# Pooled attention with a gated MLP: a bank read ahead of two sums in the last two tiles, and a sum and a load put behind the rows of x in the second tile

## Chip, core and metric

The kernel runs on one core of a Trainium2 chip. The time is the device time in microseconds (us) of one launch. Before the change nine runs had a median of 287.71 us (287.24 to 288.73).

## What is computed

The reference takes q, k and v of 8 batches, 8 heads, 576 positions and 64 channels. Keys and values are averaged over groups of 8 positions, so each head has 72 pooled keys. The result x of the attention has 4608 rows (batch by position) and 512 columns (head by channel), and goes through a gated two-layer MLP:

```
k_p = k.reshape(B, H, Sp, 8, D).mean(axis=3);  v_p likewise
attn = softmax(q @ k_p^T / sqrt(D))
x = (attn @ v_p), as 4608 rows x 512
h = x @ w_in            # 512 -> 2048
g = h * cos(h)
out = g @ w_out         # 2048 -> 512
```

## The kernel before

**Tiles.** The MLP runs over nine tiles of 512 rows, t = 0 to 8. While tile t is in the MLP, TensorE also does the attention of batch b = t + 1, whose result tile t + 1 reads. So tiles 1 to 6 are "steady" (`steady` is b < 8), tile 7 has only the last 64 rows of batch 7 left to do (`rest`), and tile 8 has none. The schedule is manual: each engine runs its instructions in the order in which the program issues them.

**Up part of a tile.** Eight groups of eight matmuls (L353) multiply the columns of `xT` (x transposed) with `w_in` into PSUM banks. For each group ScalarE takes the cosine (L363) and VectorE multiplies it with h (L367) into `g_sb`. The groups go through the banks in the order 0, 2, 1, the two output banks, 0, 2, 1, 0.

**Down part.** From tile 1 on, the product with `w_out` is made by seven half-size products instead of eight (a Strassen-like scheme), `product(0)` to `product(6)`, 16 matmuls each (L431). They need four sums of quarters of g, `put_g(1..4, i)` (L397), each in two halves i, made by VectorE: `g1` and `g3` from `g_sb`, `g2` from `g1`, `g4` from `g2`. Every product accumulates in one of two banks, A (`obanks[1]`) or Bb (`obanks[0]`; in the last tile each of them is a pair of banks, so that the two halves of the rows can be read one by one). Products alternate between the two: 0, 2, 4, 6 in A, and 1, 3, 5 in Bb. After each product `reads[i]` empties its bank, `reads[0]` by a copy to `p_sb` (L445; VectorE, in tiles 7 and 8 ScalarE), the others by an addition on VectorE (L447). Products 2 and 3 begin a new sum in their bank, so product 2 waits for `reads[0]` (and for g2), and product 3 for `reads[1]` (and for g1). Product 4 needs g3, product 5 needs g4. In tile 8 each read issues its two output DMAs for each half of the rows; in the other tiles the output DMAs come in the next tile.

**Attention in a steady tile.** The batch's first 384 rows go in three chunks u0, u1, u2. `values_rows` multiplies the exponentials with the pooled values (L295), takes reciprocals (L298) and makes the rows of x (`x_rows`, L300) on VectorE, and SyncE issues a DMA that transposes them into `xT` (L304). The next tile's first matmul waits for all three. The chunk u3 and the last 64 rows (`values`, L268 to L279) follow later in the tile.

**GpSimd.** At the end of tile t it pools the keys and then the values of batch b + 1 with `pool_first` (four additions, L156) and `pool_rest` (two additions, L162, and the writes to `ring`, L165, or to `vz`, L168). The second half for the values, `pool_rest(b, "v")`, stands in the next tile's up part. It also issues the loads: the keys of batch b + 2 by `load_kv` (L115) between the two halves of the pooling of the keys, and the q and v of the batch after next in the up part (L96, L115), behind a one-element copy `gate` (L589) that waits for the transposed keys `kk`. A second `gate` (L712), which waits for `put_g(4, 1)`, stands ahead of the pooling. SyncE issues the transposes of q (L206) and of the pooled keys (L192) in the up part too.

The order in the down part, which the change edits, is that of L664 to L681:

```
product(1, 2)
if t == 1:
    put_g(2, 0)
put_gs((1, 1), (2, 1))
reads[0]()
put_gs((3, 1), (4, 1))
reads[1]()
if t == 1:
    put_g(4, 0)
if steady:
    values_rows(*u0)
product(2)
reads[2]()
```

Of the kernel before, what the change touches and what calls it, by code (L numbers as in the profile page):

```python
# [20 lines left out]
def kernel(  # L21
# [10 lines left out]
    B, H, S, D = q.shape  # L32
# [119 lines left out]
    def pool_first(b, which):  # L152

        x, s = staged.pop((which, b)), half_sums
        for h in range(0, H, 2):
            nc.gpsimd.tensor_tensor(out=s[:, h:h + 2], in0=x[:, h:h + 2, 0:4, :], in1=x[:, h:h + 2, 4:8, :], op=ADD)  # L156
# [60 lines left out]
    def ex_col(u, i):  # L217

        (c0, n), (h0, nh) = u
        return (i // 2 % 2 * (nh // 2) + i // 4 * 2 + i % 2) * n  # L220
# [66 lines left out]
    def values_rows(b, u, pair):  # L287

        (c0, n), (h0, nh) = u
        ex = att.pop(("ex", b, u))  # L290
        ps = pair.rearrange("p b n -> p (b n)").rearrange("p (j w) -> p j w", w=2 * 128)
        for i in range(nh):
            pj, hp = divmod(i, 2)
            v_and_sum = vz[b % 2].rearrange("p j a d -> p j (a d)")[:, pj, hp * (3 * D - 1):hp * (3 * D - 1) + D + 1]
            nc.tensor.matmul(ps[0:n, pj, hp * (D + 1):(hp + 1) * (D + 1)], lhsT=ex[:, ex_col(u, i):ex_col(u, i) + n],  # L295
                             rhs=v_and_sum)
        inv = asb.tile([128, KCH, 2], FP32, name="inv_rows", tag="inv_rows", bufs=2)
        nc.vector.reciprocal(out=inv[0:n], in_=ps[0:n, :, D:D + 2])  # L298
        x = asb.tile([128, d_model], BF16, name="x_rows", tag="x_rows", bufs=4)
        nc.vector.tensor_tensor(  # L300
            out=x[0:n].rearrange("p (j a d) -> p j a d", j=KCH, a=2),
            in0=ps[0:n, :, 0:2 * (D + 2)].rearrange("p j (a w) -> p j a w", a=2)[:, :, :, 0:D],
            in1=inv[0:n].unsqueeze(3).to_broadcast([n, KCH, 2, D]), op=mybir.AluOpType.mult)
        nc.sync.dma_start_transpose(out=xT[:, :, b * S + c0:b * S + c0 + n], in_=x[0:n])  # L304
# [94 lines left out]
    def put_gs(*kis):  # L399
        for k, i in kis:  # L400
            put_g(k, i)
# [159 lines left out]
    for t in range(NT):  # L561
        b = t + 1
        if t > 0:

            for fp in up_order(t)[0:2]:
                up_mm(t, fp, 0, 2)
        for n, fp in enumerate(up_order(t)):
            up_mm(t, fp, 2 if n < 2 else 0)
            between = ()
            if t == 0:  # L570
                if fp == 4:
                    puts = pool_k_mm(1, obanks[0], 0, 2), pool_k_mm(1, obanks[1], 2, 4)
                elif fp in (5, 6):
                    g0 = 9 * (fp - 5)
                    puts = q_transpose_mm(1, obanks[0], g0, g0 + 5), q_transpose_mm(1, obanks[1], g0 + 5, g0 + 9)
                if fp in (4, 5, 6):
                    puts[0](vec)
                    between = ((puts[1], act),)
            up_g(t, fp, between)
            if 0 < t and 3 <= n < 6:  # L580
                put_gs(*[(k, 0) for k in (((3,), (1,), ()) if t == 1 else ((1, 2), (3,), (4,)))[n - 3]])
            if 0 < t and b < B:
                if n == 0:
                    q_transpose(b)
                    k_transpose(b)
                elif n == 2:
                    pool_rest(b, "v")
                    if b + 1 < B:
                        nc.gpsimd.tensor_copy(out=gate, in_=kk[b % 2][0:1, H - 1, 0:1])  # L589
                        load_q(b + 1)  # L590
                        load_kv(b + 1, "v", v)
            if n == 2:
                while stores:
                    stores.pop(0)()
        mms = [(ms, fc) for ms in range(4) for fc in range(FFCH)]
        if t == 0:
            mms = [(ms, fc) for hm in range(2) for cg in (0, 2, 1, 3) for ms in range(2 * hm, 2 * hm + 2)
                   for fc in range(4 * cg, 4 * cg + 4)]


        def S_(n, bank):
            return lambda: scores(b, us[n], banks[bank])

        later = []

        def V_(n, bank, wait=None):
            return lambda: values(b, us[n], banks[bank], wait)

        fill = []
        if t < B:  # L610
            exp_tables()
            fill = [(1, lambda: scores(t, REST, banks[2])), (16, lambda: values(t, REST, banks[1]))]
        if t == 0:
            fill = [(2, fill[0][1]), (2, S_(0, 0)), (8, lambda: pool_v_mm(1, banks[1])),
                    (8, lambda: values(t, REST, banks[2])), (8, S_(1, 0)), (8, V_(0, 1)),
                    (18, S_(2, 2)), (21, V_(1, 0, later)), (26, S_(3, 1)), (32, lambda: later.pop()()),
                    (32, V_(2, 2)), (40, V_(3, 0))]
        if t == FIRST:
            early_inverses.clear()
        if t < FIRST:  # L620
            fi = 0
            for n, (ms, fc) in enumerate(mms):
                while fi < len(fill) and fill[fi][0] <= n:
                    fill[fi][1]()
                    fi += 1
                down_mm(obanks[ms % 2], ms, fc)
                if fc == FFCH - 1:
                    down_out(t, ms, obanks[ms % 2])
                if n == 4:
                    put_weights(0, nc.vector, (1,))  # L630
                elif n == 36:
                    put_weights(1, nc.vector, (3,))
            put_weights(1, nc.vector, (2, 4))
        else:
            products, reads = down_products(t)

            def product(i, j=0, k=2 * HF):
                for mm in products[i][j:k]:
                    mm()

            later = []

            u0, u1, u2, u3 = [(b, CHUNKS[i], banks[j]) for i, j in enumerate((2, 1, 0, 1))]
            ur = (t, REST, banks[2])

            def scores_of(*parts):
                for part in parts:
                    scores_mm(*part)
                for part in parts:
                    scores_exp(*part)  # L650

            def muls():
                while later:
                    later.pop(0)()

            steady, rest = b < B, t < B
            if rest:
                exp_tables()
            product(0)
            product(1, 0, 2)  # L660
            if steady:
                scores_of(u0, u1, u2)
            elif rest:
                scores_of(ur)  # L664
            product(1, 2)
            if t == 1:
                put_g(2, 0)
            put_gs((1, 1), (2, 1))
            reads[0]()
            put_gs((3, 1), (4, 1))  # L670
            reads[1]()
            if t == 1:
                put_g(4, 0)
            if steady:
                values_rows(*u0)
            product(2)
            reads[2]()
            if steady:
                values_rows(*u1)
                values_rows(*u2)  # L680
            product(3)  # L681
            reads[3]()
            muls()
            product(4)
            reads[4]()
            muls()
            if steady:
                scores_of(ur, u3)
            product(5, 0, 4)
            if rest:  # L690
                values(*ur, later)
            product(5, 4, 12)
            muls()
            if steady:
                values_rows(*u3)
            product(5, 12)
            reads[5]()
            muls()
            product(6)
            reads[6]()  # L700
        if t < B:
            sin_tables()
        if b + 1 < B:
            if t == 0:
                load_kv(b + 1, "k", k)
                load_q(b + 1)
                load_kv(b + 1, "v", v)
                put_weights(0, nc.gpsimd, (3, 2, 4))
                put_weights(1, nc.gpsimd, (1,))
            else:  # L710

                nc.gpsimd.tensor_copy(out=gate, in_=g4[0:1, HF - 1, 0:1])  # L712
            pool_first(b + 1, "k")
            if b + 2 < B:
                load_kv(b + 2, "k", k)
            pool_rest(b + 1, "k")
            pool_first(b + 1, "v")
# [1 line left out]
_INS = ['q', 'k', 'v', 'moe_w_in', 'moe_w_out']  # L719
# [26 lines left out]
```

The softmax here doesn't subtract the row's maximum and nothing guards it: scores larger than these inputs give would overflow.

## Time and profile before

| | before |
|---|---|
| median of nine runs | 287.71 us |
| the profiled execution, its time | 287.55 us |
| its span | 285.8 us |
| TensorE busy (matmul) | 274.9 us, 96% of the span |
| VectorE busy | 215.9 us, 76% |
| ScalarE busy | 164.4 us, 58% |
| GpSimd busy | 144.0 us, 50% |
| granted TensorE clock, mean | 0.997 |

The profile lists busy times of the engines, groups of instructions by line, and a chain of waits: the work that ended last, followed back step by step to what released it. PE is TensorE, PEld its weight loads, DVE VectorE, ACT ScalarE, POOL GpSimd and SP SyncE; a "q" behind a name means the engine's instruction queue. Line numbers are those of the kernel before. The span is the time between the first and the last instruction, and the 1.75 us between the span and the time of that execution lie around it.

### The profile page before, as it was taken

The numbers are of one execution on the slowest core, as the hardware profiler recorded it, in microseconds if no ns is written. First come the engines' busy times: TensorE is split into PE (matmuls) and PEld (weight loads), VectorE is DVE, ScalarE is ACT, GpSimd is POOL, SyncE is SP. The second block draws the span as 40 slices with busy tenths as digits, with TensorE's granted clock in tenths as the row PEclk, the third lists the DMA queues.
The fourth block names the chain that finished last, engine by engine and source line by source line (L and its number), as shares of the span: only waits on it lengthen the run. The fifth ranks groups of instructions, "written<-read, shape, count | busy, mean of one in ns | idle before, by whom it ended". The sixth has DMA issues, their size and how long they took to land.

```text
span 285.8 us, 5835 instructions
## 1 busy us (share of the span) xinstructions
PE 274.9 (96%) x2338; PEld 176.3 (62%) x2360; DVE 215.9 (76%) x314; ACT 164.4 (58%) x193; POOL 144.0 (50%) x150
## 2 busy tenths in 40 slices
PE   7889999999999999999999999999999999999994
PEld 2645454446864597458745874587458845874683
DVE  5458747999947995799569956995699569747972
ACT  3886798367157735673567456745665566337600
POOL 8553079995699259925993499349900000000000
PEclk9999999999999999999999999999999999999998
DMA  7999999794789987997779867882660261015014
GB/s 153 204 207 206 207 205 216 127 187 66 127 115 131 170 169 118 131 179 146 112 134 164 168 101 145 156 174 42 124 147 8 53 141 24 2 35 112 2 37 110
DMA packets 57737, 36.12 MB, mean 126 GB/s; under 512 B 35440, under 2 KB 53360, under 8 KB 57712
## 3 DMA queue, kind: packets, MB, share of 16 engines
q0 software_dynamic: 19744, 18.07, 40.7%
q1 hardware_dynamic: 37328, 17.18, 29.2%
q10 hardware_dynamic: 640, 0.52, 0.8%
q8 instruction: 18, 0.29, 0.4%
q14 instruction: 7, 0.06, 0.1%
HBM read 36.70 MB, written 9.44 MB: 161 GB/s over the span
## 4 chain that ended last, share of the span: by engine, by line
PE 80%; DVE 10%; ACT 4%; DMA 3%; issue 2%; DVEq 0%; ACTq 0%
PE bank L353 35%; PE obank L431 27%; PE obank L370 4%; PE obank L353 4%; DVE g_sb L367 3%; PE bank L233 3%; DVE g L397 3%; ACT cos L363 2%; PE bank L295 2%; DMA xT<-x_rows 1%; PE bank L268 1%; DVE w L387 1%; DMA g_sb<-in_k_dram 1%; PE bank L431 1%; ACT ex L240 1%
## 5 line engine op out<-in xcount | busy, mean ns | idle before, releaser
L353 PE MATMUL bank<-xT,w_in_sb 128*128 128x512 bf16 x495 | 113.1, 379 | 1.5 <-DMA xT<-x_rows 0.5
L363 ACT ACTIVATE cos<-bank,half_pi 128x1024 f32<-128x1024 f32 x64 | 70.4, 1114 | 57.5 <-PE bank L353 56.6
L353 PEld LDWEIGHTS <-w_in_sb 128*128 128x128 bf16 x576 | 56.1, 98 | 66.8 <-issue 1.5
L367 DVE TENSOR_TENSOR g_sb<-bank,cos 128x1024 bf16<-128x1024 f32 x64 | 77.3, 1220 | 25.7 <-ACT cos L363 25.6
L156 POOL TENSOR_TENSOR half_sums<-kv_st 72x512 f32<-72x512 bf16 x48 | 54.8, 1169 | 0.7 <-issue 0.2
L240 ACT ACTIVATE ex<-bank 72x1024 bf16<-72x1024 f32 (+1 forms) x40 | 35.0, 929 | 33.8 <-PE bank L233 33.8
L431 PEld LDWEIGHTS <-g 128*128 128x128 bf16 x512 | 47.9, 98 | 7.0 <-issue 1.2
L431 PE MATMUL obank<-w,g 128*128 128x256 bf16 x368 | 42.8, 272 | 0.3 <-DVE p_sb L445 0.2
L431 PEld LDWEIGHTS <-g_sb 128*128 128x128 bf16 x384 | 36.7, 98 | 6.8 <-DVE g_sb L367 0.2
L162 POOL TENSOR_TENSOR half_sums<-half_sums 72x512 f32<-72x512 f32 x24 | 30.5, 1291 | 0.1
L431 PE MATMUL obank<-w_out_sb,g_sb 128*128 128x256 bf16 x240 | 28.9, 273 | 0.0
L397 DVE TENSOR_TENSOR g<-g_sb 128x1024 bf16<-128x1024 bf16 x32 | 23.3, 727 | 0.5
L712 POOL COPY gate<-g 1x1 bf16<-1x1 bf16 x5 | 0.9, 182 | 37.1 <-DVE g L397 37.1
L279 DVE TENSOR_TENSOR xT<-bank,inv 64x256 bf16<-64x256 f32 x14 | 5.9, 422 | 15.2 <-ACT inv L275 15.1
L300 DVE TENSOR_TENSOR x_rows<-bank,inv_rows 128x512 bf16<-128x512 f32 x24 | 16.6, 692 | 0.8
L431 PE MATMUL obank<-w_out_sb,g 128*128 128x256 bf16 x112 | 15.6, 273 | 0.0
L431 PE MATMUL obank<-w,g_sb 128*128 128x256 bf16 x128 | 15.3, 273 | 0.0
L370 PE MATMUL obank<-w_out_sb,g_sb 128*128 128x512 bf16 x61 | 14.8, 379 | 0.4 <-issue 0.3
L353 PE MATMUL obank<-xT,w_in_sb 128*128 128x512 bf16 x64 | 15.1, 379 | 0.0
L233 PE MATMUL bank<-qT,kk 64*72 64x128 bf16 (+2 forms) x288 | 12.6, 221 | 0.1
L233 PEld LDWEIGHTS <-kk 64*72 64x72 bf16 x288 | 8.9, 110 | 5.2 <-issue 4.0
L331 ACT ACT_TABLE_LOAD x9 | 11.5, 1283 | 0.9 <-PEq L730 0.8
(103 smaller groups left out, 277.2 us busy)
## 6 DMA issues: line engine op xcount, KB each, us to landing
out_dram<-o_two SPq DMA_DIRECT2D x64, 128.0 KB, 2.4
kv_st<-in_v_dram POOLq DMA_DIRECT2D x8, 576.0 KB, 11.3
kv_st<-in_k_dram POOLq DMA_DIRECT2D x7, 576.0 KB, 8.3
q_b<-in_q_dram POOLq DMA_DIRECT2D x6, 576.0 KB, 7.6
w_in_sb<-in_moe_w_in_dram POOLq DMA_DIRECT2D x4, 512.0 KB, 13.1
w_out_sb<-in_moe_w_out_dram POOLq DMA_DIRECT2D x4, 512.0 KB, 18.7
q_b<-in_q_dram POOLq DMA_DIRECT2D x4, 288.0 KB, 12.0
g_sb<-in_k_dram SPq DMA_DIRECT2D x1, 576.0 KB, 3.7
```

What stands on the lines that cost most here:

```text
L156: nc.gpsimd.tensor_tensor(out=s[:, h:h + 2], in0=x[:, h:h + 2, 0:4, :], in1=x[:, h:h + 2, 4:8, :], op=ADD)
L162: add(out=s[:, h:h + 4, 0:2, :], in0=s[:, h:h + 4, 0:2, :], in1=s[:, h:h + 4, 2:4, :], op=ADD)
L233: nc.tensor.matmul(pair[:Sp, bank, c:c + n].rearrange("p (g n) -> p g n", n=64), lhsT=kk[b % 2][half[r], key_slot(b, h0 + i, r), 0:Sp], rh ...
L240: nc.scalar.activation(out=ex[:, 0:nh * n].rearrange("p (a n) -> p a n", a=2), in_=pair[:Sp, :, 0:nh * n // 2], func=ACTF.Exp, scale=scale ...
L300: nc.vector.tensor_tensor(out=x[0:n].rearrange("p (j a d) -> p j a d", j=KCH, a=2), in0=ps[0:n, :, 0:2 * (D + 2)].rearrange("p j (a w) -> ...
L331: nc.scalar.preload_act_table_set("natural_log_exp_and_others")
L353: nc.tensor.matmul(h[j] if h is obanks else h[:, j, :], lhsT=w_in_sb[fc // 4][:, ki, (fc % 4) * 128:(fc % 4 + 1) * 128], rhs=xT[:, ki, t * ...
L363: nc.scalar.activation(out=c, in_=ps, func=ACTF.Sin, bias=half_pi[:, :1])
L367: nc.vector.tensor_mul(out=o, in0=ps, in1=c)
L370: nc.tensor.matmul(o, lhsT=g_sb[:, fc, ms * 128:(ms + 1) * 128], rhs=w_out_sb[fc // 4][:, fc % 4, :], start=(fc == 0), stop=(fc == FFCH - 1))
L397: nc.vector.tensor_tensor(out=out[:, f0:f1], in0=x, in1=y, op=op)
L431: mms.append(lambda bank=bank, first=first, g=g, w=w, fc=fc, p=p: nc.tensor.matmul(bank[p], lhsT=g(fc, p), rhs=w(fc), start=(first and fc ...
```

## The change

Two edits in the down part, one at the tile's end. In tiles 7 and 8 `reads[1]` is issued ahead of `put_gs((3, 1), (4, 1))`. In tile 1 `values_rows(*u0)` is issued ahead of `put_g(4, 0)`. In tile 1 the load of the keys of batch 4 is issued behind `pool_rest(3, "k")` and not ahead of it. Tiles 2 to 6 keep their order.

```
             put_gs((1, 1), (2, 1))
             reads[0]()
+            if not steady:
+                reads[1]()
             put_gs((3, 1), (4, 1))
-            reads[1]()
+            if steady:
+                reads[1]()
+                values_rows(*u0)
             if t == 1:
                 put_g(4, 0)
-            if steady:
-                values_rows(*u0)
             product(2)
             reads[2]()
...
             pool_first(b + 1, "k")
-            if b + 2 < B:
+            if t != 1 and b + 2 < B:
                 load_kv(b + 2, "k", k)
             pool_rest(b + 1, "k")
+            if t == 1:
+                load_kv(b + 2, "k", k)
             pool_first(b + 1, "v")
```

On the engines this changes three places in the order of VectorE (tile 1: the reciprocal and the rows of u0 ahead of one sum; tile 7: one read ahead of two sums; tile 8: the read's two halves ahead of two sums) and one in that of GpSimd (the load behind two L162 and two L165). The orders of TensorE, ScalarE and SyncE stay the same.

## The prediction

> **What bounds the kernel now.** I read the page first: TensorE is busy 96% of the span at a granted clock of 0.997, so time can only come from the places where it stands. The list of waits from the second tile on names three on TensorE, 0.2 to 0.5 us each. The chain of waits shows them in place: ahead of tile 2, in tile 7 and in tile 8 (start, us, what).
>
> ```profile
> 78.85 4.21 DMA xT<-x_rows
> 83.07 0.14 issue
> 83.20 0.38 PE bank L353
> ...
> 246.97 0.61 DVE o_two L447
> 247.58 0.04 issue
> 247.63 4.09 PE obank L431 x36
> ...
> 273.89 0.68 DVE o_two L447 x2
> 274.56 0.04 issue
> 274.61 1.80 PE bank L431 x15
> ```
>
> In tile 1 the transpose of u2, issued at 78.85, lands 4.21 us later, and tile 2 begins with it. In tiles 7 and 8 `reads[1]` (`o_two`) ends last ahead of product 3. Then the timeline of VectorE, GpSimd and TensorE around these places (start, duration, engine, line):
>
> ```profile
> 62.24 2.95 POOL L162 TENSOR_TENSOR half_sums<-half_sums 72x512 f32<-72x512 f32 x2
> 62.24 1.81 DVE L397 TENSOR_TENSOR g<-g_sb 128x1024 bf16<-128x1024 bf16 x1
> ...
> 73.79 0.68 DVE L397 TENSOR_TENSOR g<-g_sb,g 128x1024 bf16<-128x1024 bf16 x1
> 73.82 5.00 POOL L156 TENSOR_TENSOR half_sums<-kv_st 72x512 f32<-72x512 bf16 x4 [0.23 <-issue]
> ...
> 79.12 0.85 POOL L115 DMA_DIRECT2D kv_st<-in_k_dram  x1 [0.30 <-POOL half_sums L156]
> ...
> 91.23 1.26 POOL L168 TENSOR_TENSOR vz<-half_sums 72x512 bf16<-72x512 f32 x1
> 92.18 0.86 DVE L397 TENSOR_TENSOR g<-g_sb 128x1024 bf16<-128x1024 bf16 x1
> ...
> 98.43 0.55 PEld L431 LDWEIGHTS <-g_sb 128*128 128x128 bf16 x6 [0.22 <-DVE g_sb L367]
> ```
>
> A sum on VectorE takes 0.68 us, but 1.81 where GpSimd starts an addition at the same moment (62.24), and 0.86 where L168 is still running (92.18). Where the sum is there first (73.79), GpSimd pays: four L156 take 5.00 us, in other tiles 4.49. So these sums and GpSimd's additions exclude each other. The last line is TensorE's small wait in tile 2, for VectorE.
>
> **Tile 7.** Product 2 starts at 245.60 and runs 16 x 0.109 = 1.75 us, to 247.35; product 3 starts at 247.63. Cost of the wait: 0.28 us. VectorE now makes g1 (244.35), g2 (245.08), g3 (245.69), g4 (246.29), each 0.60 behind the one before, and reads at 246.89. With the read third it can start when product 1 has ended (245.60, plus the 0.19 that q_sb shows between the end of product 3 and its read: 249.38 to 249.57) and the copy by ScalarE too (245.44): 245.79. It ends at 246.47, 0.9 us ahead of 247.35. The wait goes whole. What is late next: g3 would end at about 247.1 and g4 at 247.7, but product 4 begins only at 249.1 and product 5 at 250.9; `v_sb` behind them starts at 247.59 instead of 247.55, and its bank is wanted at 249.1. All of that is covered. The read's extra waits, for output DMAs of its old buffer, cost nothing: those end before 238. Gain 0.28.
>
> **Tile 8.** Product 2 starts at 272.15 and would be followed by product 3 at 273.90 and product 4 at 275.65. Now product 3 starts at 274.28 with the first half of the read, goes on at 274.61 with the second, and product 4 starts at 276.24. Cost: 0.59 us. After the change the halves are read from 272.60 (VectorE is free of g2 then) to 273.35, so product 3 starts at 273.90; g3 ends at about 274.0 and g4 at 274.6, wanted at 275.65 and 277.40; `v_sb` keeps its 274.47, because the same work lies ahead of it. The eight output DMAs of that read are issued about 1.2 us earlier, from both queues, which move nothing between 262 and 274.25. From there TensorE runs to the end, so the gain reaches the end: 0.59. No GpSimd work is left in either tile (its row of slices is 0 there), so the exclusion above cannot touch these sums.
>
> **Tile 1, the load.** Once the transposes are in time TensorE would start tile 2 directly behind product 6, which starts at 80.75; in tile 2 that step takes 110.40 to 112.15, 1.75 us. So 82.50 instead of 83.20: at most 0.70. u2's transpose is late by the load of the keys. Its packets flow from 80.1; between 81 and 83 the transposes' queue moves 31 packets while the load's queue, which begins at 80.95, moves 319:
>
> ```profile
> q0 software_dynamic: 319, 0.15, 74.2%
> q1 hardware_dynamic: 31, 0.00, 1.8%
> ```
>
> With the load behind the pooling it is issued at about 83.0, and its data starts some 1.8 us later (79.12 to 80.95 now). The transpose of u2, issued at 78.85 as before, then takes the usual 2.5 us: 81.35, 1.15 us ahead of 82.50. The page "DMA: Bandwidth & Descriptors" of the Trainium skill (section "Queues, rings and completion order") speaks against this part: each DMA engine is said to take its queues in turn, a packet at a time. By that, 31 packets beside 319 would be done in some 0.2 us and the load would not be the cause, so moving it would bring nothing; the row of 31 packets in two microseconds decides for the other reading here.
>
> **Tile 1, the sum behind u0's rows.** The rows of u0 come 0.60 earlier. That frees nothing by itself, since u2's rows (77.59) wait for TensorE, and u2's issue (78.85) has over a microsecond of room. The sum moves from 73.79 to 74.63. There GpSimd is in its first L156 (73.82 plus 1.12, to 74.94), so the sum waits about 0.3 (bounds 0, if it slips in between, and 1.12, by the row of 62.24). `v_sb`, now 75.23 to 75.91, is pushed by that, and product 4 wants its bank at 76.11. With 0.15 of room (0.20 less 0.05 for the release) the price on TensorE is 0.16, at worst 0.97. So tile 2 starts at about 82.66 (82.50 to 83.47): 0.54 earlier, between 0.70 earlier and 0.27 later. g4 itself is wanted only at 78.4.
>
> **Tile 2, what is late next.** VectorE's first sum there (92.18) would come about 0.5 us earlier and meet L168, whose time hangs on GpSimd's own chain since 73.82 and not on TensorE. That chain gets shorter by the 0.30 that the load waits for the L156 ahead of it, and by some 0.06 of gaps (in tile 6, which has no load, L162 follows L156 without a gap): 0.36 in all, so L168 ends near 92.13 instead of 92.49. From that sum on VectorE runs without idle time to the L367 for which the weights of 98.43 wait. So TensorE cannot pass that point more than 0.36 earlier than now, whatever was won at 82.50. (The point has a wait of 0.12 now, by 2.09 us for 18 matmuls against 1.97 in tile 3, so 0.24 won at the start is enough to reach this limit.) I take 0.36 for tile 1's part; its bounds are 0.82 (0.70 and the 0.12, if L168 is out of the way) and -0.27.
>
> **The sum.** 0.28 + 0.59 + 0.36 = 1.23 us. Against the profiled execution: 287.55 - 1.23 = 286.32; the median lies 0.16 above that execution, so 286.5 us. Differences under about 0.2%, 0.58 us, can't be told from none here.
>
> **Rivals.**
> 1. *The exclusion costs nothing in tile 2.* If L168 ends earlier than I think, or the sum passes ahead of it, all of tile 1 counts: 0.28 + 0.59 + 0.82 = 1.69, 286.0 us. For it: three collisions only stand in the trace, and GpSimd's spans are rough. Against it: 92.18 shows just this meeting.
> 2. *Tile 1 wins nothing.* The sum runs into a whole L156, or GpSimd's chain keeps its length because the load waits 0.30 at its new place as well. Then only the two last tiles count: 287.71 - 0.87 = 286.84 us.
> 3. *The reads do not do what the change says.* Product 3 waits for something else in tiles 7 and 8. The trace shows no later releaser than `o_two`, so this is weak: 287.71 - 0.36 = 287.35 us.
> 4. *Slower: the load starves the transposes of tile 2.* Its data would now flow to about 91, beside the transposes of q (issued 84.30) and of the pooled keys (89.23). The copy `gate` behind the latter (93.02), and with it the loads of q and v, would come later, and the v load, which ends at about 105.3 now, would run into the transposes of x issued at 104.31 to 107.03; the load of keys of that tile, issued at 107.90, then follows at once and holds them. If u2's last packets wait for that load (8.1 us to land in tile 1), they land at about 115.4 instead of 109.5, TensorE would want them at 111.8, and tile 3 starts 3.3 us later than now: 287.71 + 3.3 - 0.87 = 290.1 us. It decides only if the gate is over some 3 us late; the transposes of q keep their issue and move 1000 packets per us when alone, so I expect 1 to 2 us.
>
> **How the numbers follow.** Forecast 0.55; rival 1 0.18; rival 2 0.13; rival 3 with "nothing changes" 0.05; rival 4 0.07; 0.02 for anything else slower. The forecast's own bounds are 286.0 to 287.1 (tile 1's part 0.82 to -0.27). Rivals 1 and 2 lie at these bounds or within. With 0.1 us below for the spread, the range is 285.9 to 287.1, and leaves out rivals 3 and 4 and the rest, 0.14. Faster by over 0.2% means below 287.13: forecast, rivals 1 and 2, 0.86, plus a small part of rival 3: 0.87. Within: 0.05. Slower: 0.08.
>
> **What would show it.** Right: no wait of TensorE on `o_two` in tiles 7 and 8, product 3 of tile 7 1.75 us behind product 2, and in tile 8 the same; tile 2's first L353 1.75 to 1.95 us behind product 6; the sum of tile 1 at about 74.6 with over 0.7 us; in tile 2 the first sum longer than 0.86 us and the weights' wait on `g_sb` longer than 0.22. Wrong: product 3 still released by VectorE; tile 2 still released by the DMA of x; a first sum of 0.68 in tile 2 (rival 1); or a DMA of x ahead of tile 3 in the chain (rival 4).

## The result, and the profile after

The changed kernel takes 286.39 us (median of 19 runs; 287.92 in the 63 runs of the kernel before beside them). The ratio is 0.9953, 95% interval 0.9941 to 0.9965: faster by 0.47%, some 1.35 us. The two profiled executions differ by 1.53 us (287.55 and 286.02), their spans by 1.6. The forecast was 286.5, the range 285.9 to 287.1. Ratios here leave out executions over 1.5% above the fastest of their kernel. The granted clock has no part in it: its mean of 0.997 before comes from the last 3.8 us (0.80 there), in which TensorE has no work left.

The chain of waits of the changed kernel (start, us, what) has only TensorE at the three places:

```profile
80.42 2.19 PE obank L431 x20
82.61 0.22 PE bank L353
82.83 0.05 issue
82.88 4.91 PE bank L353 x22
...
243.47 7.31 PE obank L431 x66
...
271.38 1.75 PE obank L431 x16
273.13 1.75 PE bank L431 x16
274.88 1.75 PE obank L431 x16
```

No transpose stands between tile 1's last product and tile 2's first L353; in tile 7 the products run on in one piece of 66; in tile 8 products 2, 3 and 4 follow each other by 1.75 us. The timeline around tile 1's end and in tile 2 (start, duration, engine, line):

```profile
73.71 4.93 POOL L156 TENSOR_TENSOR half_sums<-kv_st 72x512 f32<-72x512 bf16 x4 [0.23 <-issue]
74.52 0.88 DVE L397 TENSOR_TENSOR g<-g_sb,g 128x1024 bf16<-128x1024 bf16 x1
...
78.61 2.49 POOL L162 TENSOR_TENSOR half_sums<-half_sums 72x512 f32<-72x512 f32 x2
...
82.67 0.85 POOL L115 DMA_DIRECT2D kv_st<-in_k_dram  x1
...
90.58 1.27 POOL L168 TENSOR_TENSOR vz<-half_sums 72x512 bf16<-72x512 f32 x1
91.43 0.96 DVE L397 TENSOR_TENSOR g<-g_sb 128x1024 bf16<-128x1024 bf16 x1
...
97.77 0.55 PEld L431 LDWEIGHTS <-g_sb 128*128 128x128 bf16 x6 [0.32 <-DVE g_sb L367]
```

The sum of tile 1, now at 74.52, takes 0.88 instead of 0.68; L162 follows the additions without the old gap; L168 starts 0.65 us earlier; tile 2's first sum meets it all the same (0.96), and the weights' wait on `g_sb` has grown from 0.22 to 0.32.

Single executions differ by some tenths before tile 1, where first loads arrive (0.10 us between these two), so I compare steps inside the traces. P is the start of product 2 in tile 1, T2 and T3 the first L353 of tiles 2 and 3; "tile 7" is the step from its first L353 to that of tile 8. The first four experiments edit the kernel before, the others the changed one (e12 repeats the change; left out are e8, which shifts product 2 itself, and e11, a repetition of e4 that is read by its chain below).

| run | product 6 to T2 | T2 to T3 | P to T3 | L168 after P | tile 7 | ratio, 95% interval |
|---|---|---|---|---|---|---|
| before | 2.45 | 28.95 | 40.03 | 19.11 | 26.92 | 1 |
| the change | 1.75 | 29.04 | 39.47 | 18.56 | 26.63 | 0.9953 (0.9941 to 0.9965) |
| e1 reads | 2.71 | 28.94 | 40.27 | 19.08 | 26.64 | 0.9979 (0.9966 to 0.9992) |
| e2 load | 1.75 | 29.15 | 39.52 | 18.61 | 26.91 | 1.0001 (0.9985 to 1.0017) |
| e3 sum | 1.74 | 29.52 | 39.94 | 19.02 | 26.91 | 0.9994 (0.9982 to 1.0005) |
| e4 reads, load | 1.75 | 29.15 | 39.52 | 18.60 | 26.64 | 0.9975 (0.9952 to 0.9997) |
| e5 longer pooling | 1.75 | 29.88 | 40.32 | 19.80 | 26.63 | 0.9983 (0.9959 to 1.0007) |
| e6 shorter pooling | 1.74 | 28.95 | 39.37 | 16.46 | 26.64 | 0.9958 (0.9945 to 0.9970) |
| e7 load later | 1.75 | 29.16 | 39.60 | 18.68 | 26.64 | 0.9951 (0.9933 to 0.9970) |
| e9 load in tile 2 too | 1.74 | 29.05 | 39.48 | 18.57 | 26.64 | 0.9949 (0.9931 to 0.9966) |
| e12 the change again | 1.74 | 29.04 | 39.46 | 18.55 | 26.64 | 0.9953 (0.9936 to 0.9970) |

### The profile page after: what moved, and what is told of

It is laid out like the page before. It is cut to its first block, busy times and chain, and to the rows that moved or that the text cites. A ratio compares the mean times of both kernels' runs of the same rounds, so it can differ in the third digit from the quotient of the medians.

```text
span 284.2 us, 5835 instructions
## 1 busy us (share of the span) xinstructions
PE 274.5 (97%) x2338; PEld 176.5 (62%) x2360; DVE 215.5 (76%) x314; ACT 164.5 (58%) x193; POOL 144.3 (51%) x150
## 4 chain that ended last, share of the span: by engine, by line
PE 82%; DMA 12%; POOL 2%; DVE 1%; issue 1%; ACT 0%; POOLq 0%
PE bank L353 34%; PE obank L431 32%; DMA w_out_sb<-in_moe_w_out_dram 6%; DMA w_in_sb<-in_moe_w_in_dram 5%; PE obank L353 5%; PE obank L370 4%; PE bank L233 3%; PE bank L295 2%; PE bank L431 2%; PE bank L268 1%; DVE g L397 1%; POOL q_b L96 1%; POOL w_in_sb L124 1%; DVE g_sb L367 0%; POOL kv_st L96 0%
## 5 line engine op out<-in xcount | busy, mean ns | idle before, releaser
L353 PE MATMUL bank<-xT,w_in_sb 128*128 128x512 bf16 x495 | 112.9, 379 | 0.9
L353 PEld LDWEIGHTS <-w_in_sb 128*128 128x128 bf16 x576 | 56.1, 98 | 65.8 <-DMA w_in_sb<-in_moe_w_in_dram 0.2
L156 POOL TENSOR_TENSOR half_sums<-kv_st 72x512 f32<-72x512 bf16 x48 | 54.8, 1168 | 0.6 <-issue 0.2
L162 POOL TENSOR_TENSOR half_sums<-half_sums 72x512 f32<-72x512 f32 x24 | 30.4, 1289 | 0.1
L353 PE MATMUL obank<-xT,w_in_sb 128*128 128x512 bf16 x64 | 15.1, 379 | 0.0
L233 PE MATMUL bank<-qT,kk 64*72 64x128 bf16 (+2 forms) x288 | 12.5, 221 | 0.2
L233 PEld LDWEIGHTS <-kk 64*72 64x72 bf16 x288 | 9.0, 110 | 5.2 <-issue 4.0
```

The costliest lines, as they stand in the source:

```text
L162: add(out=s[:, h:h + 4, 0:2, :], in0=s[:, h:h + 4, 0:2, :], in1=s[:, h:h + 4, 2:4, :], op=ADD)
L233: nc.tensor.matmul(pair[:Sp, bank, c:c + n].rearrange("p (g n) -> p g n", n=64), lhsT=kk[b % 2][half[r], key_slot(b, h0 + i, r), 0:Sp], rh ...
L353: nc.tensor.matmul(h[j] if h is obanks else h[:, j, :], lhsT=w_in_sb[fc // 4][:, ki, (fc % 4) * 128:(fc % 4 + 1) * 128], rhs=xT[:, ki, t * ...
```

## Experiments: the three edits apart

**e1_reads.** Only the reads of tiles 7 and 8.

```
+            if not steady:
+                reads[1]()
             put_gs((3, 1), (4, 1))
-            reads[1]()
+            if steady:
+                reads[1]()
```

> The kernel before with the reads of tiles 7 and 8 ahead of the two sums, and nothing else. The prediction's theory: 0.28 us in tile 7 and 0.59 in tile 8, 0.87 us in all, so about 0.9970 of the time before; product 3 follows product 2 by 1.75 us in both tiles, and tile 2 still starts behind the late transpose (the step from product 6 to the first L353 is 2.45 us). Rival (the reads do not do what the change says): product 3 waits for something else, 1.000.

Measured 0.9979; 0.9970 lies in the interval. The traces give the size: tile 7 takes 26.64 instead of 26.92 us, and in tile 8 products 2, 3 and 4 follow at 1.75. Tile 2 still waits for u2, here even a little longer (4.39 us to land). The reads do what the change says.

**e2_load.** Only the load.

```
-            if b + 2 < B:
+            if t != 1 and b + 2 < B:
                 load_kv(b + 2, "k", k)
             pool_rest(b + 1, "k")
+            if t == 1:
+                load_kv(b + 2, "k", k)
```

> The kernel before with the load of the keys in tile 1 behind the pooling, and nothing else. Theory A (the load holds u2's last packets): u2 is issued at about 78.85 as before and lands 2.5 us later, tile 2 starts 1.75 us behind product 6, and what is kept behind tile 2 is what GpSimd's shorter chain allows, 0.4 to 0.6 us: about 0.9983. Theory B (the earlier rows of u0 make the transposes punctual): the load's place does nothing, tile 2 starts 2.4 us behind product 6, 1.000.

u2, issued at 78.80, lands 2.4 us later; tile 2 starts 1.75 us behind product 6, and 0.51 us is left at tile 3 (39.52 against 40.03). That is theory A by the trace. The time does not show it: the ratio is 1.0001, and 0.9983 lies just outside the interval. The profiled execution itself took 287.11 us, against 287.55. What other executions lost is not seen in that trace; e11 below shows one way in which it can happen.

**e3_sum.** Only the sum behind u0's rows.

```
             reads[1]()
+            if steady:
+                values_rows(*u0)
             if t == 1:
                 put_g(4, 0)
-            if steady:
-                values_rows(*u0)
```

> The kernel before with the sum of tile 1 behind the rows of u0, and nothing else. Theory A (as predicted, the earlier rows free nothing by themselves): u2 is issued at about 78.8 and lands some 4.2 us later, tile 2 starts as late as before, 1.000 to 1.0005. Theory B: u0's transpose is issued 0.6 us earlier, u2's follows at about 78.2 and lands in 2.5 us, ahead of the load's data; tile 2 starts 1.75 us behind product 6. But GpSimd's chain keeps its length, the first sum of tile 2 takes about 1.5 us, and behind tile 2 at most 0.1 to 0.2 us are left: 0.9995.

Theory B, and my own statement about this edit falls. The chain of waits of this kernel:

```profile
80.95 2.19 PE obank L431 x20
83.14 0.22 PE bank L353
...
91.96 1.45 DVE g L397
93.41 0.02 issue
93.43 0.69 DVE g L397
...
97.59 1.15 DVE g_sb L367
98.73 0.05 issue
98.78 0.83 PE obank L431 x6
```

Tile 2 starts on time although the load stands in its old place. But L168 starts 19.02 us behind P, only 0.09 earlier than before, and now VectorE's first sum comes just behind its start (91.57) and takes 1.45 us. VectorE is then the chain up to 98.73, and tile 2 takes 29.52 instead of 28.95 us. Of the 0.66 us that T2 comes earlier behind P only 0.09 is left at T3; the ratio, 0.9994, cannot be told from 1. Either edit alone ends the late transpose; only the load's move also shortens GpSimd's chain by much (0.50 us in e2).

**e4_reads_load** and **e11_reads_load_again.** Reads and load, without the sum's move, twice.

> The changed kernel without the move of the sum in tile 1 (reads and load only). Theory A: the sum's move adds nothing, so the ratio is that of the whole change, 0.9953, or a little better, since product 4 of tile 1 is not held (0.05 us). Theory B: the sum's move is needed, the ratio is that of the reads alone, 0.9970.

> Reads and load only, a second time, beside the whole change on the same chip. By the traces the sum's move is worth 0.06 us (0.50 us kept behind tile 2 against 0.56), so the two should agree within the interval. If the earlier rows of u0 keep the transposes of tile 2 out of the load's way in some executions, this kernel is slower by 0.2% or more, and has more single slow runs.

Measured 0.9975 (0.9952 to 0.9997) and 0.9946 (0.9928 to 0.9965): the same kernel, so the ratios alone leave open whether the sum's move adds anything. By the traces e4 keeps 0.51 us behind tile 2 and the change 0.56. The other half of e11's expectation, more single long executions, fits the counts: of the 32 executions of the kernels that move the load without the sum (e2, e4, e11) six took over 289 us, of the 92 of the other kernels in the same two rounds none. How the sum's move would work against them is not shown.

**e12_change_again.**

> The whole change a second time, beside reads and load only on the same chip: 0.9953 again, and, by the traces, 0.06 us (0.02%) less than that kernel.

0.9953 again; P to T3 is 39.46 us, 0.06 less than in e4.

## Experiments: what limits tile 2

**e5_long_pool.** One addition more in the pooling of the values in tile 1.

```
-        for h in range(0, H, 2):
+        for h in [0] * more + list(range(0, H, 2)):   # more = 1 for the values of tile 1
```

> The changed kernel with one more L156 (the first pair of heads added a second time) in the pooling of the values in tile 1: GpSimd's chain is 1.12 us longer, nothing else changes. Theory (L168 sets when VectorE's first sum of tile 2 can run, and that sets TensorE): L168 ends about 1.1 us later, the first sum of tile 2 takes about 2.0 us instead of 0.96, the step from tile 2's first L353 to tile 3's grows from 29.04 to about 30.1 us. Rival (GpSimd's chain is covered): no change, 29.04.

The timeline of this kernel:

```profile
91.68 0.85 DVE L397 TENSOR_TENSOR g<-g_sb 128x1024 bf16<-128x1024 bf16 x1
92.06 1.60 POOL L168 TENSOR_TENSOR vz<-half_sums 72x512 bf16<-72x512 f32 x1
92.56 1.65 DVE L397 TENSOR_TENSOR g<-g,g_sb 128x1024 bf16<-128x1024 bf16 x1
...
95.40 1.89 PE L353 MATMUL bank<-xT,w_in_sb 128*128 128x512 bf16 x8 [0.45 <-DVE g_sb L367]
```

L168 starts 19.80 us behind P, 1.24 later. It is now the second sum that meets it (1.65 us), and TensorE waits for VectorE already in the up part. Tile 2 takes 29.88 us, 0.84 more; I had expected 1.1, since I had let the first sum wait for the whole of L168. Of the 1.24 us by which GpSimd's chain grows, 0.84 reach TensorE.

**e6_short_pool.** Two of those four additions left out (half of the sums of the values of batch 3 are then not made).

> The changed kernel with only two of the four L156 in the pooling of the values in tile 1, which leaves out half of that addition: GpSimd's chain is 2.25 us shorter. Theory: the first sum of tile 2 takes 0.69 us, the weights' wait on g_sb is gone, the step from tile 2's first L353 to tile 3's is 28.95 us as in the later tiles instead of 29.04. Rival (the wait in tile 2 comes from VectorE's own work): still 29.04.

```profile
88.88 1.27 POOL L168 TENSOR_TENSOR vz<-half_sums 72x512 bf16<-72x512 f32 x1
...
91.83 0.69 DVE L397 TENSOR_TENSOR g<-g_sb 128x1024 bf16<-128x1024 bf16 x1
```

L168 is over at 90.15, the sum takes 0.69, the weights' wait is gone, and tile 2 takes 28.95 us, as predicted. So in the changed kernel 0.09 us (29.04 - 28.95) is still lost there, too little for the ratio to show.

**e8_more.** Two sums placed anew, to win that and the 0.23 that tile 1's product 2 waits for the copy.

```
-                put_gs(*[(k, 0) for k in (((3,), (1,), ()) if t == 1 else ((1, 2), (3,), (4,)))[n - 3]])
+                put_gs(*[(k, 0) for k in (((3,), (1,), ()) if t == 1 else
+                                          ((1, 2), (3,), (4,) if t > 2 else ()))[n - 3]])
...
-            put_gs((1, 1), (2, 1))
-            reads[0]()
+            put_g(1, 1)
+            if t == 1:
+                reads[0]()
+            put_g(2, 1)
+            if t != 1:
+                reads[0]()
...
             put_gs((3, 1), (4, 1))
+            if t == 2:
+                put_g(4, 0)
```

> The changed kernel with two sums placed anew: in tile 2 the first half of g4 behind the second halves of g3 and g4, ahead of the second bank's read, and in tile 1 the copy of the first bank ahead of the second half of g2. Theory: tile 1's product 2 no longer waits for the copy (0.23 us), and the L367 that held TensorE in tile 2 comes 0.6 us earlier, so that wait goes too and tile 2 keeps what tile 1 won: 28.95 us for tile 2, 0.3 us in all against the changed kernel, 0.9943. Rival: the wait in tile 1 is only passed on to product 2's second half or to GpSimd's gate, 0.9953.

0.9960 (0.9946 to 0.9974): the rival; the 0.9943 of the theory lies just outside. Both waits are gone from their places. In tile 1 product 4 waits 0.16 for `v_sb` instead; in tile 2 the down part begins with 1.96 us for 18 matmuls, as in later tiles, but products 3 and 4 take 3.58 instead of 3.50, and tile 2 keeps its length (29.03).

## Experiments: the loads and the rows of x in tile 2

**e9_load_two.** The load behind the pooling in tile 2 as well (`t in (1, 2)`).

> The changed kernel with the load of the keys behind the pooling in tile 2 as well. In the runs with the load moved the rows of x in tile 2 travel at 105 to 108.5 us, held by the v load ahead of them and with the load of keys close behind. Theory (the load of keys in tile 2 catches them in some executions, which makes single runs of 288 to 293 us): no such runs here, and the profile as for the changed kernel, 0.9953 or a little better. Rival: the outliers come from somewhere else and stay, or the late load makes tile 3's loads late in turn and something waits there.

0.9949, not to be told from the change, and the profile is the same (39.48). One execution of 291.69 us is among its runs all the same, and one of 291.41 us among those of the kernel before beside it, so such executions cannot be put down to tile 2's load of keys alone.

**e7_load_late.** The load of tile 1 behind the first half of the pooling of the values.

```
-            if t == 1:
-                load_kv(b + 2, "k", k)
             pool_first(b + 1, "v")
+            if t == 1:
+                load_kv(b + 2, "k", k)
```

> The changed kernel with the load of the keys in tile 1 another four additions later, behind the first half of the pooling of the values. Issued at about 87.1 us, its data flows from 88.9 to 95, so it meets the transposes of the pooled keys; the gate behind them comes at about 96 to 97 instead of 94.55, the v load of tile 2 ends near 108.5 instead of 106.7, and the load of keys of tile 2 follows at 109. Theory of rival 4 (past a point the loads catch the rows of x of tile 2): u2's transpose lands only when that load is done, tile 3 starts 1 to 4 us late, slower than before. Rival theory (the queues take turns once both flow, so the transposes pass): u2 lands by 111, tile 3 on time, 0.995.

The gate came at 96.74, as expected and 3.7 us later than before, but tile 3 starts on time and the ratio is 0.9951. The transposes of q, issued ahead of the load, took 2.66 us to issue instead of 5.96, and the v load was done before 107, not at 108.5. So a gate over 3 us late does not by itself bring rival 4's loss.

That loss exists all the same. The profile of e11 (291.05 us) happened to catch it; the timeline and the chain of waits of that execution:

```profile
97.81 0.18 POOL L589 COPY gate<-kk 1x1 bf16<-1x1 bf16 x1 [5.54 <-DMA kk<-ring]
99.17 0.83 POOL L115 DMA_DIRECT2D kv_st<-in_v_dram  x1
...
107.52 7.07 DMA xT<-x_rows
114.58 0.25 issue
114.83 7.03 PE bank L353 x24
```

The gate is 4.8 us later than before (93.02): the transposes of q took 8.32 us to issue, so those of the pooled keys came only at 94.03. The v load is still flowing past 108, u2's transpose, issued at 107.5, lands 7.07 us later, and tile 3 starts 4.22 us behind product 6, 2.47 later than it should. This is rival 4 link by link. One more loss was in no rival: TensorE had stood 2.31 us, and from 115.6 to 118.6 its granted clock was 0.50, so that the first 24 L353 took 7.03 instead of 5.34 us. That is another 1.7 us. Why the issue took so long in that execution and not in others was not settled, and whether the pause brought the lower clock is not shown by this one case.

## Why the prediction was right, point by point

**Tile 7.** 0.28 predicted; 26.92 - 26.63 = 0.29 measured, and 0.28 in e1.

**Tile 8.** 0.59 predicted. From T8 (254.85 and 253.91) to product 4 (276.24 and 274.71) it is 21.39 and 20.80 us: 0.59 measured. The read ran where it was put (271.67), and no later step took the gain back.

**Tile 1 to tile 3.** 0.36 predicted, 0.56 measured (40.03 - 39.47). The mechanism was right: tile 2 starts on time, VectorE's first sum there meets L168, and part of the gain is given back; e5 and e6 move this limit both ways. In six kernels what T3 wins behind P is, to 0.01 us, what L168 wins: 0.56 and 0.55 in the change, 0.51 and 0.50 in e2, 0.09 and 0.09 in e3, 0.51 and 0.51 in e4, 0.43 and 0.43 in e7, 0.55 and 0.54 in e9. Two terms were mis-sized, both to the small side, so no error covered another: the steps sum to 0.29 + 0.59 + 0.56 = 1.44 us against the 1.23 of the prediction. The stall of product 4 was put at 0.16; the sum waited 0.20 and not 0.3, so TensorE lost 0.05. GpSimd's chain was to get 0.36 shorter; it got 0.55 shorter (19.11 to 18.56): 0.35 for the wait of the load and the gap behind it, 0.11 for the gaps around L165, which I had not counted, and 0.07 because the sum now cost the four L156 less (4.93 instead of 5.00). The 0.12 us at the weights of 98.43 was misread: the 24 matmuls behind them (L233) take 0.79 us there and 0.91 in tile 3, which makes up for it, and tile 2 took 28.95 us before, no more than tile 3 (28.94). So the upper bound was not 0.82. With L168 out of the way, e6, it is 0.66 (40.03 - 39.37).

**The sum behind u0's rows "frees nothing by itself".** Wrong, as e3 shows. I took u2's issue, 78.85, for set by u2's rows. It was set by SyncE's queue: u0's issue took 2.11 us before and held u1 to 77.54, while u1's rows were ready at 76.75. The issue of u0 before and in e3:

```profile
75.34 2.11 SPq L304 DMA_TRANSPOSE xT<-x_rows  x1
...
75.17 1.19 SPq L304 DMA_TRANSPOSE xT<-x_rows  x1
```

In e3 u0 is issued 0.60 us earlier behind P and its issue takes 1.19, so u2 follows 0.59 earlier behind P and lands 2.5 us later. The changed kernel has the same times behind P. The step did no harm to the sum, because the load's move alone brings the transposes in time too (e2).

**The rivals.** Rival 1 would need 28.95 us for tile 2: not reached, and by e6 its price was 0.66 and not 0.82, so 286.2 us. Rivals 2 and 3 fall with P to T3 and with tiles 7 and 8. Rival 4: I expected the gate 1 to 2 us late; it came 1.53 late (94.55), the rows of x of tile 2 moved at 35 to 254 packets per us until the v load's end and at 1006 in the microsecond after it, and u2's last packets moved in the microsecond in which the next load began (236 packets from 108 to 109). The margin was thinner than I had it. The condition "over some 3 us late" did not hold as it stands: e7 was 3.7 us late without a loss.

**The page on DMA.** The rule of the Trainium skill that each DMA engine takes its queues in turn, a packet at a time ("DMA: Bandwidth & Descriptors", section "Queues, rings and completion order"), was set against 31 packets in two microseconds. In the changed kernel the transposes of q and the load flow side by side from 87 to 90:

```profile
q0 software_dynamic: 345, 0.35, 72.1%
q1 hardware_dynamic: 437, 0.11, 59.4%
```

That is far nearer to even than 31 against 319, and does not speak against the page. But in e11, with transposes of x under way beside the v load, the queues moved 45 and 191 packets from 107 to 108. So these runs do not settle the rule, and what held u2's last 31 packets while the load began is not explained by them. That the load held them is shown by e2.

## What to carry to other kernels

When a stall is taken away, follow the engine that would be next to the first place where it meets an independent chain, here GpSimd's; what is won is at most what that chain allows, and lengthening and shortening that chain shows it quickly. In a group of sums with different due times, read out first the bank that the next product waits for: it costs nothing where the sums have slack. A moved load should be judged twice, once where it left and once where it now flows.

## What was not expected of the hardware

- A sum on VectorE with both inputs in SBUF and an addition on GpSimd hold each other up, for about what is left of one instruction: the sum took 0.68 us alone and 0.85 to 1.81 where GpSimd was at work first, and GpSimd's L168 took 1.60 instead of 1.27 where the sum was first (e5). The page "SBUF — State Buffer" of the Trainium skill (section "Who interferes with whom") says that a VectorE instruction with two SBUF inputs contends with a GpSimd instruction that reads SBUF, and calls this an exclusive lock; these rows agree.
- The issue of u0's transpose on SyncE took 1.19 us in every profile in which u0's rows came ahead of the sum, and 2.0 to 2.2 us in every one in which they came behind it, for the same transfer; the longer one was enough to delay the two later transposes by 0.6 us. Why it is longer is open.
- The transpose of q (18 blocks) in tile 2 took 2.66 us to issue in e7, where the load of keys came behind it, and 4.06 to 8.32 us elsewhere, with that load beside it.
- In e11 TensorE's granted clock was 0.50 for some 3 us behind a pause of 2.31 us, and matmuls that take 5.34 us took 7.03.
